# Residual written to the output early, results added by accumulating stores, and three buffer pools of the last stage laid over other places

## The chip, the cores and the metric

The kernel runs on one core of a Trainium2 chip. The time is the device time of one execution in microseconds (us). Before the change it is 1024.56 us, the median of three runs (1024.05 to 1024.94).

## The reference

Two branches are computed on the same LayerNorm of the input and added to the input itself. `x` has 2048 tokens (S) of 640 features (D); the hidden size F is 1728.

```python
xn = _layernorm(x, axis=-1)
# FNet: real part of a DFT over features and tokens
a = xn @ dft_hid_re.T ; b = xn @ dft_hid_im.T
fnet = dft_seq_re @ a - dft_seq_im @ b
# gated unit
gate = xn @ W_gate ; up = xn @ W_up
h = where(gate > 0, gate, 0) * up
return x + fnet + h @ W_down
```

All is float32.

## The kernel before

**Arithmetic.** A float32 matrix is split into a high part (rounded to the matmul's fp32r type) and a low part (the rest). `split` makes them: ScalarE (ACT) copies the high part, VectorE (DVE) subtracts it. `mm3` (lines 139 to 141) then does three matmuls of 128 x 128 by 128 x 512 for each product on TensorE (PE). The large products use a two-by-two block scheme with seven products instead of eight (names T1 to T4, S1 to S4, B11 to B22), so sums and differences of blocks are formed ahead of the matmuls, and results are added in several places afterwards.

**Stages.** Phase 1 (about 0 to 400 us) streams the sequence DFT matrices (`raw`, `tk`) over the tokens. `stream(c, name, g)` (around line 690) is one step of it: `load` issues the DMA of a 512 KB block on SyncE's queue (SP), `prepare` sums and splits, `run` multiplies. Phase 2 (about 400 to 731 us) computes `gate_up(n)` for 26 blocks n of F. A unit takes 12.2 us: it loads raw weights `z` (`Weights(n + 2)`, line 855), splits them into `gw`, runs seven block products, copies some of them from the matmul banks with ACT (`p`, `ob`, `u`: the copy must be done before PE adds the next product to the same bank), and stores the gated result `ob` to `hd` with GpSimd's queue (POOL). In the same phase, weights of the last stage are packed: loaded as `pw`, summed and stored as `wparts` (line 1060). Phase 3 (about 731 to 1019 us) multiplies the packed weights `wt` with rows `rw` and `ro` of the two branches: `project(1)`, then `project(0)`, with small further steps (`second_level`, called quads) between them.

**The last stage's steps.** `unit(name, u, first, last)` in `project` returns `load` (issue the DMA of `rw` or `ro`), `fetch` (issue the DMA of `wt`), `prepare` (differences and splits) and `run` (matmuls). `drive_last` calls `fetch`, `load`, `prepare` and `run` of successive units each some units apart (AHEAD 6, ROWS 6, READY 3). Its order is binding for SP, POOL and PE, and a scheduler places the instructions of ACT and DVE, which may land in phase 2. In phase 2 PE, DVE and ACT are bound and the scheduler places SP. Each engine works its instructions in order, and an SP or POOL instruction that waits holds back the ones behind it.

**Places.** The pools of the last stage are laid over memory of phase 2. A load into such a place waits for the last reader of what lay there before. Before the change, from the left: `low` (rows B12) over gate weights and stage, `gap`, `wts` (seven buffers for `wt`) over `r1` and part of `prep`, `lead` (six for rows B11) over the rest of `prep` and `z`, `ring2`, `raws`; from the right: `odd` (for `ro`) over gate weights, and `y`. `prep` holds the `pw` tiles until their packing stores have landed.

**Results.** The output is out = x + fnet + gated unit, transposed: 5 row blocks e of 128 features by 4 chunks of 512 tokens (q and c). `get_y` (line 1212) loads a 256 KB block of `xt`, the residual, into a place `y`. `add_y` (lines 1217 and 1219) adds one finished bank to it on DVE; when all additions to that block are done it is stored, by POOL two steps later (line 1229, `defer`) or by SP where `late` is set (line 1227). The last block is stored in two halves by ACT and SP (line 1225).

Of the kernel before, what the change touches and what calls it, by code (L numbers as in the profile page):

```python
# [10 lines left out]
OP = mybir.AluOpType  # L11
# [54 lines left out]
def fnet_reglu_kernel(  # L66
# [625 lines left out]
    def stream(c, name, g):  # L692
        t = {}
        sub = lambda o, i0, i1: nc.vector.tensor_tensor(o, i0, i1, op=OP.subtract)

        def get(m, half, o=None):
            o = raw() if o is None else o
            late["dma"] = nc.sync.dma_start(o, dft[c, m, half * NH + g]).ins
# [48 lines left out]
        todo.append((load, prepare, run, lambda: combine(c, name) if g == NH - 1 else None))  # L747
# [450 lines left out]
    y, missing, ends = {}, {}, []  # L1198

    for q in range(2):  # L1200
        for e in range(KD):
# [12 lines left out]
    def add_y(q, e, c, ps, late=False, op=OP.add, at=slice(0, CH), queue=None):  # L1214
        t = y[q, e, c][:, at]
        if op == OP.add:
            nc.vector.tensor_tensor(t, ps, t, op=OP.add)  # L1217
        else:
            nc.vector.tensor_tensor(t, t, ps, op=op)
        missing[q, e, c] -= 1  # L1220
        if missing[q, e, c] == 0 or queue is not None:
            first = (2 * q + c) * CH
            o = out[e * P : (e + 1) * P, first + at.start : first + at.stop]
            if queue is not None:
                queue.dma_start(o, t)
            elif late:
                nc.sync.dma_start(o, t)
            else:
                defer(1, lambda: nc.gpsimd.dma_start(o, t))

    def project(q):
        c0, c1 = 2 * q, 2 * q + 1
# [6 lines left out]
        def get(kind, u):  # L1239
            what, ks = UNITS[u]  # L1240
            if what == "odd":
                o = raws[kind, u] = pool("odd").tile([P, 1, CH], F32, name="ro")
            else:
                o = raws[kind, u] = pool({"B11": "lead", "B12": "low"}.get(kind, "raws")).tile([P, 2, CH], F32, name="rw")[:, : len(ks)]
# [12 lines left out]
        def unit(name, u, first, last):  # L1257
# [19 lines left out]
            def fetch():  # L1277
                if name == "B11" and (q, u) == (1, 0):
                    return
                t["w"] = w = pool("wts").tile([P, 2, 2, 3 * P], F32R, name="wt")[:, :n]  # L1280
                put = lambda o, i: nc.sync.dma_start(o.bitcast(F32), i)
                sums = wparts[:, k0 : k0 + n]
                if name in PARTS:
# [99 lines left out]
            begin = lambda: put_off.pop()()  # L1383
            return load, prepare, run, fetch

        LOADS_Y = {"B11": ((0, 0), (1, 0), (4, 1), (4, 0)) if q else ((4, 1),), "T1": ((2, 1), (3, 1)), "T2": ((0, 1), (1, 1)), "T4": ((2, 0), (3, 0))}

        def read(name):
            two = range(2)
            if name == "B11":  # L1390
# [13 lines left out]
            for e, c, key in todo:  # L1404
                if name == "T4" and q == 0 and e == 3:
                    for ps, j in ends:
                        add_y(q, e, c, ps, at=slice(j * HC, (j + 1) * HC), queue=(nc.scalar, nc.sync)[j])
                else:
                    add_y(q, e, c, B[key], late=q == 0 and name in ("T3", "T4"))

        steps = []
        for name, us in (("B11", every), ("T1", every), ("T2", every), ("B22", every[:4]), ("T3", every), ("B22", every[4:]), ("T4", every)):
            for u in us:
# [8 lines left out]
                loaded = "B11" if q and (name, u) == ("T1", 0) else name if u == 3 and (q, name) != (1, "B11") else None  # L1422
                if loaded in LOADS_Y:
                    step.append(alone((lambda which: lambda: get_y(q, *which))(LOADS_Y[loaded])))
                steps.append((step, (q, name, u)))
        return steps

    def second_level():
# [4 lines left out]
        def unit(name, g):  # L1433
# [11 lines left out]
                nc.sync.dma_start(t["r"], src)  # L1445

            def fetch():
                t["w"] = w = pool("wts").tile([P, 2, 6 * P], F32R, name="wt")[:, :n]
# [60 lines left out]

    alone = lambda f: (f, idle, idle, idle, idle)  # L1510
    quads = second_level()
    Y_AFTER = {(1, "T2", 5): ((4, 0),), (1, "T4", 5): ((0, 0), (1, 0))}
    for q in (1, 0):
        for steps, of in project(q):
            todo.extend(steps)
            if of in Y_AFTER:
                todo.append(alone((lambda which: lambda: get_y(0, *which))(Y_AFTER[of])))
# [47 lines left out]
```

## Time and profile before

One execution was profiled. All its records are of core 0.

| | us |
|---|---|
| the profiled execution's own time | 1024.17 |
| its span in the trace | 1022.4 |
| PE busy | 1016.7 |
| DVE busy | 824.4 |
| ACT busy | 455.5 |
| POOL busy | 117.3 |

The granted TensorE clock was 1.00 in all 40 slices of the span. The DMA engines were busy for 62 to 93% of the time in the windows used below. In lists of groups a row names line, engine, operation, output and input tiles and count, then the busy time and the mean of one in ns, then the idle time of the engine just before them with what ended it. In timelines the columns are start, duration, engine, line, operation, tiles, count, and in brackets the idle time before with its releaser. SPq is SyncE's sequencer issuing DMAs; a weight split stands there as `wt<-wt` on ACT, line 133, and on DVE, line 134.

### The profile page before, as it was taken

To read this page: it belongs to the slowest core of one execution; us is meant where nothing else is said; L and a number is where in the kernel's file an instruction comes from. 1 tells how busy PE (TensorE), PEld (TensorE's weight loads), DVE (VectorE), ACT (ScalarE), POOL (GpSimd) and SP (SyncE) were. 2 spreads that over 40 slices of the span, in tenths; PEclk is the share of its full clock that TensorE was granted. 3 is DMA by queue.
4 is the path that set the end of the run, shared out by engine and by line. 5 is a ranking of instruction groups with operands and counts; after the bars stand their busy time and mean duration, and the time that the engine had idled before them with its cause. 6 is when DMAs were issued, how large, how long until landed. Compare 5 with 4: busy or idle time off the path is not lost. (4 is left out here: it accounts for less than half of the span.)

```text
span 1022.4 us, 12767 instructions
## 1 busy us (share of the span) xinstructions
PE 1016.7 (99%) x4510; PEld 841.6 (82%) x4510; DVE 824.4 (81%) x1162; ACT 455.5 (45%) x588; POOL 117.3 (11%) x189
## 2 busy tenths in 40 slices
PE   9999999999999999999999999999999999999998
PEld 8888888888888888888888888888788888888887
DVE  7967976969989697788888977877487888599877
ACT  6664453333334443434445544443353454444552
POOL 2000010121110002321111111111100000000001
PEclk9999999999999999999999999999999999999999
DMA  9884744966859566764658999988698879999685
GB/s 331 320 283 157 266 147 142 332 252 205 356 200 345 218 199 217 255 231 171 234 209 282 284 311 309 308 335 266 188 399 249 257 250 328 327 314 322 216 286 167
DMA packets 113872, 267.57 MB, mean 262 GB/s; under 512 B 13104, under 2 KB 58096, under 8 KB 112176
## 3 DMA queue, kind: packets, MB, share of 16 engines
q1 hardware_dynamic: 92416, 179.03, 51.7%
q0 software_dynamic: 20960, 87.31, 24.8%
q8 instruction: 35, 0.57, 0.2%
q10 hardware_dynamic: 432, 0.43, 0.1%
q14 instruction: 29, 0.24, 0.1%
HBM read 203.26 MB, written 72.89 MB: 270 GB/s over the span
## 5 line engine op out<-in xcount | busy, mean ns | idle before, releaser
L140 PE MATMUL ps<-cb,wt 128*128 128x512 f32 (+1 forms) x407 | 158.0, 388 | 0.0
L139 PE MATMUL ps<-cb,wt 128*128 128x512 f32 (+1 forms) x407 | 157.9, 388 | 0.0
L141 PE MATMUL ps<-cb,wt 128*128 128x512 f32 (+1 forms) x407 | 157.9, 388 | 0.0
L133 ACT ACTIVATE cb<-rw 128x1024 fp32r<-128x1024 f32 (+1 forms) x94 | 89.2, 960 | 78.8 <-PE ps L141 54.7
L134 DVE TENSOR_TENSOR cb<-rw,cb 128x1024 fp32r<-128x1024 f32 (+1 forms) x94 | 102.7, 1101 | 21.6 <-ACT cb L133 20.6
L133 ACT ACTIVATE cb<-raw 128x1024 fp32r<-128x1024 f32 x64 | 67.9, 1061 | 105.1 <-PE ps L141 94.9
L134 DVE TENSOR_TENSOR cb<-raw,cb 128x1024 fp32r<-128x1024 f32 x64 | 78.1, 1221 | 31.5 <-ACT cb L133 31.1
L139 PE MATMUL ps<-xs_early,gw 128*128 128x512 f32 x260 | 101.3, 389 | 1.0 <-ACT ob L130 1.0
L140 PE MATMUL ps<-xs_early,gw 128*128 128x512 f32 x260 | 101.2, 389 | 0.0
L141 PE MATMUL ps<-xs_early,gw 128*128 128x512 f32 x260 | 101.2, 389 | 0.0
L139 PE MATMUL ps<-cb,xs_late 128*128 128x512 f32 x232 | 90.2, 389 | 0.0
L140 PE MATMUL ps<-cb,xs_late 128*128 128x512 f32 x232 | 90.2, 389 | 0.0
L141 PE MATMUL ps<-cb,xs_late 128*128 128x512 f32 x232 | 90.2, 389 | 0.0
L140 PEld LDWEIGHTS ps<-cb,wt 128*128 128x128 f32 x407 | 76.4, 188 | 15.9 <-DVE cb L134 0.3
L139 PEld LDWEIGHTS ps<-cb,wt 128*128 128x128 f32 x407 | 76.4, 188 | 15.8
L141 PEld LDWEIGHTS ps<-cb,wt 128*128 128x128 f32 x407 | 76.4, 188 | 15.8
L140 PE MATMUL ps<-cb,xs_early 128*128 128x512 f32 x226 | 87.9, 389 | 0.0
L139 PE MATMUL ps<-cb,xs_early 128*128 128x512 f32 x226 | 87.9, 389 | 0.0
L141 PE MATMUL ps<-cb,xs_early 128*128 128x512 f32 x226 | 87.9, 389 | 0.0
L130 ACT ACTIVATE gw<-z 128x1024 fp32r<-128x1024 f32 (+1 forms) x52 | 56.4, 1109 | 38.5 <-PE ps L141 22.2
L130 ACT ACTIVATE u<-ps 128x512 f32<-128x512 f32 x52 | 31.1, 597 | 88.3 <-PE ps L141 70.9
L875 DVE TENSOR_TENSOR gw<-z,gw 128x1024 fp32r<-128x1024 f32 (+1 forms) x52 | 64.8, 1284 | 1.9 <-ACT gw L130 1.8
(209 smaller groups left out, 1991.6 us busy)
## 6 DMA issues: line engine op xcount, KB each, us to landing
raw<-in_dft SPq DMA_DIRECT2D x94, 512.0 KB, 5.4
wt<-wparts SPq DMA_DIRECT2D x74, 256.0 KB, 4.4
wparts<-pw POOLq DMA_DIRECT2D x12, 1408.0 KB, 6.6
z<-in_wgu SPq DMA_DIRECT2D x26, 640.0 KB, 5.4
rw<-hd SPq DMA_DIRECT2D x27, 512.0 KB, 6.7
hd<-ob POOLq DMA_DIRECT2D x26, 512.0 KB, 4.1
wt<-wparts SPq DMA_DIRECT2D x29, 384.0 KB, 5.8
rw<-pq SPq DMA_DIRECT2D x19, 512.0 KB, 6.4
```

The costliest lines, as they stand in the source:

```text
L130: return nc.scalar.activation(o, i, AF.Copy)
L133: nc.scalar.activation(hi, src, AF.Copy)
L134: return nc.vector.tensor_tensor(lo, src, hi.bitcast(F32), op=OP.subtract)
L139: nc.tensor.matmul(ps, wh, mh, start=first, stop=False, skip_group_check=more)
L140: nc.tensor.matmul(ps, wh, ml, start=False, stop=False, skip_group_check=more)
L141: nc.tensor.matmul(ps, wl, mh, start=False, stop=last, skip_group_check=more)
L875: tt(self.w[:, 1, cs], self.z[:, cs], self.w[:, 0, cs].bitcast(F32), op=OP.subtract)
```

## The change

Three things are edited.

1. The residual goes to the output in phase 1: five copies of 1 MB from `xt` to `out`, on SP's queue, in the load step of five units of the first chunk (`XT_AT`). 18 of the 20 loads of `y` are dropped. The first result for a block is now copied from its bank by ACT (with factor −1 where it is subtracted), later ones are added by DVE as before, and the finished block is stored by POOL with an adding DMA. Two blocks, (q 0, e 2, c 0) and (q 0, e 3, c 0), are still loaded (`load_plain`) and stored plainly, the last of them in two halves.
2. Two stores of q = 0, which SP issued, are issued by POOL.
3. The pools of the last stage get other places. From the left now: `odd`, `y0`, `gap`, `wts0` (five buffers), `wts1` (two), `y1`, `lead0` (five), `ring2`, `lead1` (one), `low`, `raws` (16 instead of 15); from the right `y2`. `in_two` hands out the buffers of `wts` and `lead` in turn over their two pools.

```diff
+XT_AT = (("T3", 1), ("T3", 3), ("T4", 0), ("T4", 1), ("T4", 2))
...
         def load():
+            if c == 0 and (name, g) in XT_AT:
+                e = XT_AT.index((name, g))
+                nc.sync.dma_start(out[e * P : (e + 1) * P], xt[e * P : (e + 1) * P])
...
-    for n, b, side in (("low", 6, "left"), ("gap", 1, "left"), ("wts", AHEAD + 1, "left"), ("lead", 6, "left"), ("ring2", 4, "left"), ("raws", 15, "left"),
-                       ("odd", 4, "right"), ("y", 1, "right")):
+    for n, b, side in (("odd", 4, "left"), ("y0", 1, "left"), ("gap", 1, "left"), ("wts0", 5, "left"), ("wts1", AHEAD - 4, "left"),
+                       ("y1", 1, "left"), ("lead0", 5, "left"), ("ring2", 4, "left"), ("lead1", 1, "left"), ("low", 6, "left"),
+                       ("raws", 16, "left"), ("y2", 1, "right")):
...
+    Y_AT = {n: "y0" if i < 8 else "y1" if i < 9 else "y2" for i, n in enumerate("001 101 401 41 01 11 21 31 20 30 000 100 400".split())}
+    turns = {"wts": [0, AHEAD + 1], "lead": [0, 6]}
+
+    def in_two(name):
+        turns[name][0] += 1
+        return pool(name + str(int((turns[name][0] - 1) % turns[name][1] >= 5)))
...
-    def get_y(q, *which):
-        for e, c in which:
-            own = f"{q}" if e in (0, 1, 4) and c == 0 else ""
-            y[q, e, c] = t = pool("y").tile([P, CH], F32, name=f"y{e}{c}{own}")
-            nc.sync.dma_start(t, xt[e * P : (e + 1) * P, (2 * q + c) * CH : (2 * q + c + 1) * CH])
...
+    def add_y(q, e, c, ps, op=OP.add, at=slice(0, CH), queue=None):
+        o = out[e * P : (e + 1) * P, (2 * q + c) * CH + at.start : (2 * q + c) * CH + at.stop]
+        missing[q, e, c] -= 1
+        if (q, e, c) not in y:
+            t = place_y(q, e, c)
+            nc.scalar.activation(t, ps, AF.Copy, scale=1.0 if op == OP.add else -1.0)
         else:
-            nc.vector.tensor_tensor(t, t, ps, op=op)
...
+            t = y[q, e, c][:, at]
+            if op == OP.add:
+                nc.vector.tensor_tensor(t, ps, t, op=OP.add)
+            else:
+                nc.vector.tensor_tensor(t, t, ps, op=op)
+        if queue is not None:
+            queue.dma_start(o, t)
+        elif missing[q, e, c] == 0:
+            if (q, e, c) in PLAIN:
                 nc.sync.dma_start(o, t)
             else:
-                defer(1, lambda: nc.gpsimd.dma_start(o, t))
+                defer(1, lambda: nc.gpsimd.dma_start(o, t, accum_op=OP.add))
...
-                t["w"] = w = pool("wts").tile([P, 2, 2, 3 * P], F32R, name="wt")[:, :n]
+                t["w"] = w = in_two("wts").tile([P, 2, 2, 3 * P], F32R, name="wt")[:, :n]
```

The change moves instructions at three places that the prediction speaks of. The lists show an engine's instructions in program order; a number at the end of a tile's name only tells tiles apart.

At the end of phase 2, SP's queue before the change: the first weights, then rows and weights of the next units, and the first `ro`.

```order
L1281 DMA wt_5793<-wparts_94 128x2x384
L1253 DMA rw_5795<-pq2_88 128x1024
L1253 DMA rw_5797<-pq2_88 128x1024
L1281 DMA wt_5799<-wparts_94 128x384
L1253 DMA rw_5801<-pq2_88 128x512
L1281 DMA wt_5803<-wparts_94 128x2x384
L1255 DMA rw_5805<-hd1_91 128x2x512
L1281 DMA wt_5812<-wparts_94 128x384
L1251 DMA ro_5814<-hd1_91 128x512
L1281 DMA wt_5821<-wparts_94 128x2x384
```

And after it, the same queue at this place. `rw_5812` waits for the packing store of the second to last `pw` tile instead of the last one, `ro_5831` for the last product of unit 24 instead of the products of unit 25.

```order
L859 DMA z_5482<-in_wgu 128x1280
L1271 DMA rw_5812<-pq2_88 128x1024
L1271 DMA rw_5814<-pq2_88 128x1024
L1299 DMA wt_5816<-wparts_94 128x384
L1271 DMA rw_5818<-pq2_88 128x512
L1299 DMA wt_5820<-wparts_94 128x2x384
L1273 DMA rw_5822<-hd1_91 128x2x512
L1299 DMA wt_5829<-wparts_94 128x384
L1269 DMA ro_5831<-hd1_91 128x512
L1299 DMA wt_5838<-wparts_94 128x2x384
L1273 DMA rw_5840<-hd1_91 128x2x512
L1299 DMA wt_5847<-wparts_94 128x2x384
```

The rows and weights between the last `z` and `ro` keep their order. The first weights (`wt_5793` before) have left this place. They stand in unit 18 now, on SP behind its `z` load:

```order
L1045 DMA pw_4890<-in_wd 128x128
L1046 DMA pw_4890<-in_wd 128x256
L859 DMA z_4987<-in_wgu 128x1280
L1299 DMA wt_5810<-wparts_94 128x2x384
L1044 DMA pw_4989<-in_wd 128x256
```

ACT in that unit, first before and then after the change: the split of these weights now stands between the weights of the next unit and the copy `ob`.

```order
L130 ACTIVATE gw_4967<-z_4883 128x1024
L130 ACTIVATE gw_4967<-z_4883 128x1152
L130 ACTIVATE ob_4965<-ps_4935 128x512
L130 ACTIVATE u2_4962<-ps_4933 128x512
L130 ACTIVATE u3_4963<-ps_4933 128x512
```
```order
L131 ACTIVATE gw_4972<-z_4888 128x1024
L131 ACTIVATE gw_4972<-z_4888 128x1152
L134 ACTIVATE wt_5810<-wt_5810 128x2x384
L131 ACTIVATE ob_4970<-ps_4940 128x512
L131 ACTIVATE u2_4967<-ps_4938 128x512
```

Nothing else in that unit's order on ACT is changed.

ACT at the end of phase 2, first before, then after: three splits stand ahead of unit 25's `ob` in both, and two more now stand behind it, ahead of the copies `u2` and `u3`. Line numbers after the change are higher by 1 to 18.

```order
L130 ACTIVATE p1_5635<-ps_5611 128x512
L133 ACTIVATE wt_5799<-wt_5799 128x384
L133 ACTIVATE wt_5803<-wt_5803 128x2x384
L133 ACTIVATE wt_5812<-wt_5812 128x384
L130 ACTIVATE ob_5639<-ps_5613 128x512
L130 ACTIVATE u2_5636<-ps_5611 128x512
L130 ACTIVATE u3_5637<-ps_5611 128x512
```
```order
L131 ACTIVATE p1_5640<-ps_5616 128x512
L134 ACTIVATE wt_5816<-wt_5816 128x384
L134 ACTIVATE wt_5820<-wt_5820 128x2x384
L134 ACTIVATE wt_5829<-wt_5829 128x384
L131 ACTIVATE ob_5644<-ps_5618 128x512
L134 ACTIVATE wt_5838<-wt_5838 128x2x384
L131 ACTIVATE u2_5641<-ps_5616 128x512
L134 ACTIVATE wt_5847<-wt_5847 128x2x384
L131 ACTIVATE u3_5642<-ps_5616 128x512
```

The splits of `wt_5838` and `wt_5847` answer to those of `wt_5821` and `wt_5830`, which stood behind all of unit 25's copies.

More of the change, by code (lines that the diff above doesn't have):

```diff
@@ L1197, in fnet_reglu_kernel @@
     fixed = [bank() for _ in range(8)]
-    y, missing, ends = {}, {}, []
+    Y_AT = {n: "y0" if i < 8 else "y1" if i < 9 else "y2" for i, n in enumerate("001 101 401 41 01 11 21 31 20 30 000 100 400".split())}
[3 more added lines that the diff above has]
+        return pool(name + str(int((turns[name][0] - 1) % turns[name][1] >= 5)))
+    y, missing, ends, PLAIN = {}, {}, [], ((0, 2, 0), (0, 3, 0))
     for q in range(2):
@@ L1206, in fnet_reglu_kernel, with place_y, load_plain @@
     missing[0, 3, 0] += 2
-    def get_y(q, *which):
-        for e, c in which:
-            own = f"{q}" if e in (0, 1, 4) and c == 0 else ""
-            y[q, e, c] = t = pool("y").tile([P, CH], F32, name=f"y{e}{c}{own}")
-            nc.sync.dma_start(t, xt[e * P : (e + 1) * P, (2 * q + c) * CH : (2 * q + c + 1) * CH])
[L1214 to L1217, printed above, removed]
-        else:
-            nc.vector.tensor_tensor(t, t, ps, op=op)
[L1220 to L1226, printed above, removed]
+    def place_y(q, e, c):
+        own = f"{q}" if e in (0, 1, 4) and c == 0 else ""
+        y[q, e, c] = t = pool(Y_AT[f"{e}{c}{own}"]).tile([P, CH], F32, name=f"y{e}{c}{own}")
+        return t
+    def add_y(q, e, c, ps, op=OP.add, at=slice(0, CH), queue=None):
[4 more added lines that the diff above has]
+            nc.scalar.activation(t, ps, AF.Copy, scale=1.0 if op == OP.add else -1.0)
+        else:
+            t = y[q, e, c][:, at]
[7 more added lines that the diff above has]
+            if (q, e, c) in PLAIN:
                 nc.sync.dma_start(o, t)
             else:
-                defer(1, lambda: nc.gpsimd.dma_start(o, t))
+                defer(1, lambda: nc.gpsimd.dma_start(o, t, accum_op=OP.add))
+    def load_plain():
+        for q, e, c in PLAIN:
+            nc.sync.dma_start(place_y(q, e, c), xt[e * P : (e + 1) * P, (2 * q + c) * CH : (2 * q + c + 1) * CH])
     def project(q):
@@ L1243, in get @@
             else:
-                o = raws[kind, u] = pool({"B11": "lead", "B12": "low"}.get(kind, "raws")).tile([P, 2, CH], F32, name="rw")[:, : len(ks)]
+                o = raws[kind, u] = (in_two("lead") if kind == "B11" else pool("low" if kind == "B12" else "raws")).tile([P, 2, CH], F32, name="rw")[:, : len(ks)]
             col, row = int(kind in ("B12", "B22")), int(kind in ("B21", "B22"))
@@ L1384, in unit @@
             return load, prepare, run, fetch
-        LOADS_Y = {"B11": ((0, 0), (1, 0), (4, 1), (4, 0)) if q else ((4, 1),), "T1": ((2, 1), (3, 1)), "T2": ((0, 1), (1, 1)), "T4": ((2, 0), (3, 0))}
         def read(name):
@@ L1408, in read @@
                 else:
-                    add_y(q, e, c, B[key], late=q == 0 and name in ("T3", "T4"))
+                    add_y(q, e, c, B[key])
         steps = []
@@ L1421, in project @@
                     step.append((l, p, r, (lambda name: lambda: read(name))(kind) if last else idle, f))
-                loaded = "B11" if q and (name, u) == ("T1", 0) else name if u == 3 and (q, name) != (1, "B11") else None
-                if loaded in LOADS_Y:
-                    step.append(alone((lambda which: lambda: get_y(q, *which))(LOADS_Y[loaded])))
+                if (q, name, u) == (0, "T4", 3):
+                    step.append(alone(load_plain))
                 steps.append((step, (q, name, u)))
@@ L1447, in fetch @@
             def fetch():
-                t["w"] = w = pool("wts").tile([P, 2, 6 * P], F32R, name="wt")[:, :n]
+                t["w"] = w = in_two("wts").tile([P, 2, 6 * P], F32R, name="wt")[:, :n]
                 put = lambda o, i: nc.sync.dma_start(o.bitcast(F32), i)
@@ L1515, in fnet_reglu_kernel @@
             todo.extend(steps)
-            if of in Y_AFTER:
-                todo.append(alone((lambda which: lambda: get_y(0, *which))(Y_AFTER[of])))
             if of == (1, "T2", 6):
```

1 line of the change is left out of this document (removed).

## The prediction

> **What bounds the kernel now.** I read the page first: the busy list, then its costliest groups with the idle time before each.
>
> ```profile
> span 1022.4 us, 12767 instructions
> PE 1016.7 (99%) x4510; PEld 841.6 (82%) x4510; DVE 824.4 (81%) x1162; ACT 455.5 (45%) x588; POOL 117.3 (11%) x189
> L139 PE MATMUL ps<-xs_early,gw 128*128 128x512 f32 x260 | 101.3, 389 | 1.0 <-ACT ob L130 1.0
> ```
>
> TensorE (PE) is busy for 1016.7 of 1022.4 us. The change keeps all matmuls, so it can win only what PE does not fill: the start, a tail, and one hole, which the third row names: 1.0 us, behind ScalarE's (ACT's) copy `ob`. Next I read PE's timeline around the hole.
>
> ```profile
> 717.87 0.39 PE L141 MATMUL ps<-sets_b,gw 128*128 128x512 f32 x1
> 719.23 0.50 PE L139 MATMUL ps<-xs_early,gw 128*128 128x512 f32 x1 [0.97 <-ACT ob L130]
> 721.41 0.39 PE L139 MATMUL ps<-sets_b,gw 128*128 128x512 f32 x1
> ```
>
> It is one wait, at the end of phase 2 (the second row names it with 0.97 of the 1.0 us). A matmul starts every 1016.7 / 4510 = 0.23 us, so 719.23 − 717.87 − 0.23 = 1.13 us are lost. ACT's timeline says why, and SP's, whose queue issues the loads, says what was late before that:
>
> ```profile
> 714.68 0.53 ACT L133 ACTIVATE wt<-wt 128x384 fp32r<-128x384 f32 x1 [3.14 <-DMA wt<-wparts]
> 716.33 0.85 ACT L133 ACTIVATE wt<-wt 128x768 fp32r<-128x768 f32 x1 [1.12 <-DMA wt<-wparts]
> 718.17 0.52 ACT L133 ACTIVATE wt<-wt 128x384 fp32r<-128x384 f32 x1 [0.99 <-DMA wt<-wparts]
> 718.60 0.58 ACT L130 ACTIVATE ob<-ps 128x512 f32<-128x512 f32 x1
> ```
> ```profile
> 683.87 1.94 SPq L1281 DMA_DIRECT2D wt<-wparts  x1
> 705.09 1.69 SPq L1253 DMA_DIRECT2D rw<-pq  x2
> 709.11 0.47 SPq L1281 DMA_DIRECT2D wt<-wparts  x1
> 731.80 0.33 SPq L1251 DMA_DIRECT2D ro<-hd  x1
> ```
> ```profile
> 687.78 0.54 POOL L1060 DMA_DIRECT2D wparts<-pw  x1 [7.27 <-DMA z<-in_wgu]
> 699.98 0.56 POOL L1060 DMA_DIRECT2D wparts<-pw  x1 [6.86 <-DVE z L861]
> ```
> ```profile
> SPq L1253 <- DMA wparts<-pw: 17.8, 1, 17.8
> ```
>
> ACT works in order: three weight splits stand ahead of the `ob` copy and wait for their loads until 718.17. Without them the copy would start when its product ends: 1.16 us before PE wants it, as in unit 18 below, or 716.9. Those loads stand on SP between 705.09 and 709.11, because the row load ahead of them waited 17.8 us for the last packing store, issued at 699.98, to leave the place (`prep`) that the row overlays.
>
> **The change, part by part.**
>
> *1. Places at the boundary: removes the hole.* In the new order the first two `rw`, the three weight loads and their rows are issued behind the last `z` of phase 2 and wait for the store of 687.78, one unit sooner, and for a DVE instruction of that unit. One unit is 699.98 − 687.78 = 12.2 us, so they go out that much earlier, by 697, and even the slow loads of this place:
>
> ```profile
> wt<-wparts SPq DMA_DIRECT2D x1, 384.0 KB, 8.4
> ```
>
> (the one 384 KB weight load issued in 705 to 710, issue to landing) have landed by 706, ten before `ob` is due. Value −1.13; bounds 0 (another wait takes over) and −1.36 (the whole step from one start to the next). That is term one.
>
> *2. A new wait and a moved split at the same boundary.* `ro` now lies over gate weights and waits for the last product that reads them:
>
> ```profile
> 712.43 0.39 PE L141 MATMUL ps<-xs_early,gw 128*128 128x512 f32 x1
> ```
>
> It ends at 712.82. Queued behind `ro` on SP are a 384 KB `wt`, `rw`, `wt`, `rw`. Before they went out only after 732, so no product of phase 2 could wait for them; now the split of that first `wt` stands on ACT between `ob` and the next copy `u`, which PE needs for its matmul at 721.41, hole taken off 720.28. The copy takes 0.60 and the split 0.85 less an overlap of 0.05 to 0.1, so the load must land by 718.85. It is issued near 713.25: 5.6 us are allowed. Its rows:
>
> ```profile
> wt<-wparts SPq DMA_DIRECT2D x29, 384.0 KB, 5.8
> wt<-wparts SPq DMA_DIRECT2D x3, 384.0 KB, 8.7
> ```
>
> (the page's median, and three in 731 to 735). 5.8 costs 0.2 us of PE, 8.7 costs 3.1, and a load under 5.6 costs nothing. Fewer loads are in flight with it than at 705 or 731 (four against seven), so I take +0.4, near the median row. The second `wt` stands behind one more copy and is taken at nothing.
>
> *3. The first `wt` fetched five units earlier.* It stood at 683.87, and its split ran after `ob` and a `u` of unit 24, with nothing due behind it. Its new place is free early, so SP issues it right behind the `z` load of unit 18, and its split stands ahead of that unit's `ob`:
>
> ```profile
> 624.51 0.42 SPq L855 DMA_DIRECT2D z<-in_wgu  x1
> ```
> ```profile
> 631.26 0.60 ACT L130 ACTIVATE ob<-ps 128x512 f32<-128x512 f32 x1 [1.97 <-PE ps L141]
> ```
> ```profile
> 632.42 0.39 PE L139 MATMUL ps<-xs_early,gw 128*128 128x512 f32 x1
> ```
> ```profile
> z<-in_wgu SPq DMA_DIRECT2D x1, 640.0 KB, 5.8
> wt<-wparts SPq DMA_DIRECT2D x1, 384.0 KB, 6.2
> ```
>
> The last fence is such a pair, a `z` and the `wt` right behind it, issued in 683.3 to 684. With 6.2 us from an issue near 625.0 the weights land at 631.2, in the very moment when `ob` could start (631.26); split to 632.05, copy to 632.6, against PE's 632.42. Free if it lands by 631.0; +0.2 at 6.2; +2.7 at 8.7. I take +0.3.
>
> [...]
>
> *4. Five 1 MB copies of the residual into the output, on SP in phase 1.* The trace has no such copy. SP's longest wait, in that phase, and three windows:
>
> ```profile
> SPq L698 <- DVE cb L134: 177.4, 46, 24.1
> ```
> ```profile
> 50.00:100.00 50.00, 50.00 (x223) 41.39 (x222) 34.99 (x55) 26.86 (x39) 1.06 (x2) 1.00 0.65 224
> 100.00:200.00 100.00, 100.00 (x443) 82.81 (x442) 82.67 (x94) 42.01 (x51) 11.54 (x20) 1.00 0.62 214
> 850.00:950.00 100.00, 100.00 (x442) 82.62 (x441) 78.88 (x93) 49.79 (x64) 2.16 (x4) 1.00 0.93 322
> ```
>
> The last columns are DMA share and GB/s. 224 GB/s at a share of 0.65 is 345 at full share: an estimate of 3.0 us for 1.05 MB, 6.1 if reading and writing count apart, 15 to 30 us for five. Free in the first two windows are 17.5 + 38 = 55 us. The loads of that phase wait for places (177.4 us of SP for this line alone), not for bytes, and PE is full in both windows. Value 0; without that cover a copy delays the load behind it by up to 6 us.
>
> *5. Phase 3: 18 residual loads go, 18 adds become copies, stores accumulate.*
>
> ```profile
> y<-in_xt SPq DMA_DIRECT2D x20, 256.0 KB, 6.8
> L1217 DVE TENSOR_TENSOR y<-ps,y 128x512 f32<-128x512 f32 (+1 forms) x43 | 27.4, 670 | 4.6 <-PE ps L141 3.5 <-PE ps L1360 1.1
> L130 ACT ACTIVATE u<-ps 128x512 f32<-128x512 f32 x52 | 31.1, 597 | 88.3 <-PE ps L141 70.9
> ```
>
> VectorE (DVE) loses 18 × 0.67 = 12.1 us, ACT gains 18 × 0.60 = 10.7; both beside a full PE, worth nothing unless a bank is released late. 18 loads leave the DMA engines, five of them in the window with a share of 0.93. The 18 stores turn into accumulating ones on POOL. Landing times of its lines, minimum, median, maximum, first the plain 256 KB stores, then the accumulating 512 KB stores of phases 2 and 3:
>
> ```profile
> DMA to landing us min/median/max: 3.8/4.8/7.5
> ```
> ```profile
> DMA to landing us min/median/max: 5.1/6.9/9.2
> ```
>
> So at most 2.1 us later in the median and 1.7 in the maximum, with half the bytes. Who waits for a store? In the new order only ACT's copies of q = 0 into places that q = 1 used, and their stores are a stream of units older. Even the saturated window should see no more traffic: a load and a store become one store that reads and writes. Value 0, bounds −0.3 and +3; the gain is this one, the only other place in phase 3 where PE's weight loads wait:
>
> ```profile
> PEld ps L140 <- DVE cb L134: 0.3, 1, 0.3
> ```
>
> *6. Tail.*
>
> ```profile
> 1003.54 3.63 POOL L1229 DMA_DIRECT2D out<-y  x6 [27.69 <-DVE y L1217]
> 1018.45 0.28 PE L141 MATMUL ps<-cb,wt 128*128 128x256 f32 x1
> 1019.21 0.35 SPq L1225 DMA_DIRECT2D out<-y  x1
> ```
> ```profile
> out<-y SPq DMA_DIRECT2D x1, 128.0 KB, 2.2
> ```
>
> The last stores stay plain: 1019.21 + 2.2 = 1021.4 ends the work. Six accumulating stores from 1003.5, issued by 1009.5 at most, land by 1018.7 even at 9.2. Value 0.
>
> **Sum** against the profiled execution's own 1024.17 us (1.8 outside its span): −1.13 + 0.4 + 0.3 = −0.43, 1023.74. That execution lies 0.39 under the median of the runs, 1024.56, so for the median I add it: **1024.1**, rounded to 1024.0.
>
> **The rivals.**
> - *Loads late at the new places (slower).* Both moved splits stand ahead of copies that PE needs, with 5.6 and 6.05 us allowed. One us over costs PE one us at each. At 8.4 us (705 to 710): +2.8 and +2.4, less 1.13, is +4.1: 1028.6. Slower than the bound once both take over 7.2 us. For: 8.4 and 8.7 at this boundary. Against: those landed in a crowd of seven or more loads, which part 1 dissolves.
> - *The hole closes and nothing opens.* Loads of 5.5 us or less: −1.13, with the 0.3 of phase 3 −1.4: 1023.1. For: 5.8 is a median, half land sooner.
> - *Accumulating stores disturb the saturated window (slower).* From 835 to 881 eight of them; if each holds up the loads behind it by the 2.1 us between the medians, one or two of the places near 880 and 893 let PE wait 2 us each: +3, 1027. For: share 0.93. Against: five loads leave there.
> - *A 1 MB copy delays phase 1's loads (slower).* 6 us once, less 2 or more of lead: +4, 1028. Against: PE has no wait there.
> - *The change doesn't move the boundary.* The place of the first `rw` stays bound to the last packing store: 1024.6.
>
> **How the numbers follow.** Forecast (1023.5 to 1025.0) 0.53, hole closed only 0.19, nothing moved 0.05, loads late 0.13, stores 0.06, copies 0.04. 0.2%, about what a measurement of this kernel can tell from no change, is 2.05 us: faster than 1022.5 lies beyond the whole hole and the 0.3, hence 0.05 for a surprise, taken from the second case. Slower than 1026.6: most of the last three, 0.20. Within: 0.75. The range runs from 1022.7 (hole, 0.3 and spread of the runs) to 1026.8, where the late cases begin to count; the forecast's own is 1023.5 to 1025.0.
>
> **What would show it.** Part 1: no wait of PE for `ob` near 718, `rw` and `wt` issued by 700. Part 2: SP waiting for PE until about 713, the `wt` behind it landing between 718 and 720; if later, a wait of PE for `u` near 720. Part 3: a weight split of ACT near 631 and a wait of PE for `ob` near 632 of a few tenths. Part 4: no wait of PE from 50 to 200. Part 5: PE busy as before from 731 to 1003, landing of accumulating stores 5 to 7 us. Part 6: the last store landing 3 us after the last matmul. A PE wait of over 1 us anywhere else would make the prediction wrong.

## The result, and the profile after

The changed kernel takes 1037.82 us (median of four runs, 1035.35 to 1039.35) against 1024.75 for the kernel before: 1.0125 times as long, with a 95% interval of 1.0102 to 1.0147. The prediction was 1024.0, with a range to 1026.8. It was slower, and by more than any rival had been priced.

The profiled execution took 1035.35 us. The page's busy lines and the group that had the hole before:

```profile
span 1033.6 us, 12749 instructions
PE 1020.1 (99%) x4510; PEld 841.5 (81%) x4510; DVE 813.4 (79%) x1144; ACT 463.4 (45%) x606; POOL 124.2 (12%) x191
L140 PE MATMUL ps<-xs_early,gw 128*128 128x512 f32 x260 | 101.5, 390 | 2.9 <-ACT ob L131 2.9
```

The span grew by 11.2 us, PE's busy time by only 3.4: the matmuls are the same 4510, so PE waits 7.8 us more, and some of its matmuls are slower. Its waits (line, releaser, sum, count and longest):

```profile
PE ps L140 <- ACT ob L131: 2.9, 1, 2.9
PE ps L140 <- ACT cb L134: 2.2, 2, 1.1
PE ps L141 <- DVE cb L135: 2.0, 4, 0.5
PE ps L140 <- DVE y L1234: 1.2, 1, 1.2
```

Because both kernels run the same matmuls in nearly the same order, the start of the k-th matmul can be compared between the two traces. The difference grows in few places only. This table is worked out from the two traces: a step is the time from one matmul's start to the next after the change, less the same time before it. Places are given at the time in the kernel before.

| where | step, us | what PE waited for |
|---|---|---|
| 194.5 to 197.7 | 1.26 + 0.69 + 0.70 = 2.65 | `cb` of phase 1 |
| 632.4 | 3.04 | ACT's `ob` in unit 18 |
| just behind it | 1.71 | nothing: matmuls at a granted clock of 0.50 |
| 719.2 | −1.13 | the old hole is gone |
| 880.1 and 881.4 | 1.25 + 1.36 = 2.61 | `cb`, and the bank that `y` reads |
| 893.2 | 0.54 | `cb` |
| 929 to 935 | 0.88 | `cb` |
| the rest, small | 0.83 | |
| last matmul, 1018.45 to 1029.58 | 11.13 | |

Three separate losses, then: phase 1, unit 18, and phase 3 around 880 to 935. The profiled execution is the shortest of the four; what the other three lost beyond it, 1.7 to 4.0 us, is in no trace. I show the lines for each loss.

**Unit 18.** ACT, SP and the landings there, in the changed kernel:

```profile
628.13 0.38 SPq L1299 DMA_DIRECT2D wt<-wparts  x1
```
```profile
z<-in_wgu SPq DMA_DIRECT2D x1, 640.0 KB, 6.8
wt<-wparts SPq DMA_DIRECT2D x1, 384.0 KB, 9.0
```
```profile
637.14 0.84 ACT L134 ACTIVATE wt<-wt 128x768 fp32r<-128x768 f32 x1 [4.78 <-DMA wt<-wparts]
637.89 0.58 ACT L131 ACTIVATE ob<-ps 128x512 f32<-128x512 f32 x1
```

The split stands ahead of `ob` as foreseen, but its load needs 9.0 us instead of 6.2. Then PE's windows (busy and count of PE, PEld, DVE, ACT, POOL, then the granted clock, DMA share and GB/s):

```profile
638.50:640.00 1.50, 1.47 (x6) 1.25 (x7) 0.48 (x1) 0.46 (x1) 0.00 (x0) 0.97 0.24 81
640.00:643.40 3.40, 3.40 (x9) 2.62 (x9) 1.68 (x4) 0.00 (x0) 0.00 (x0) 0.51 0.85 226
643.40:650.00 6.60, 6.60 (x30) 5.45 (x29) 4.97 (x12) 4.05 (x5) 0.54 (x1) 1.00 0.62 249
```

After the wait PE runs at full speed for 1.4 of the 1.5 us of the first row, then 3.4 us at a granted clock of 0.51, then at 1.00 again. The nine matmuls of the second row take the time of some fifteen.

**Phase 1.** DVE in the changed kernel (first fence), and before (second):

```profile
190.58 0.69 DVE L567 TENSOR_TENSOR sa<-ps,sa 128x512 f32<-128x512 f32 x1 [1.71 <-PE ps L142]
191.30 0.69 DVE L570 SCALAR_TENSOR_TENSOR sb<-sb,sa 128x512 f32<-128x512 f32 x1
191.94 0.69 DVE L567 TENSOR_TENSOR sa<-ps,sa 128x512 f32<-128x512 f32 x1
192.66 0.69 DVE L570 SCALAR_TENSOR_TENSOR sb<-sb,sa 128x512 f32<-128x512 f32 x1
193.27 1.22 DVE L695 TENSOR_TENSOR raw<-raw,tk 128x1024 f32<-128x1024 f32 x1
```
```profile
189.56 1.22 DVE L694 TENSOR_TENSOR raw<-raw,tk 128x1024 f32<-128x1024 f32 x1
190.70 1.22 DVE L134 TENSOR_TENSOR cb<-raw,cb 128x1024 fp32r<-128x1024 f32 x1
191.83 1.28 DVE L566 TENSOR_TENSOR sa<-ps,sa 128x512 f32<-128x512 f32 x2
```
```profile
194.61 1.06 ACT L134 ACTIVATE cb<-raw 128x1024 fp32r<-128x1024 f32 x1 [7.00 <-DVE raw L695]
```

DVE now does the four `sa` and `sb` additions ahead of the difference `raw - tk`. They wait 1.71 us for a product of PE, and the difference that PE's next weights come from stands in line behind them. ACT (third fence, changed kernel) stands idle for 7.0 us until it is there. Before, the difference of 189.56 was made ahead of the additions. The difference of 193.27 has no wait of its own, so no load that it needs was late, and the last of the five copies had landed by 181.4: the order of DVE's work makes PE wait here, not the copies' traffic.

**Phase 3.** The DMA queues in equal stretches of 70 us, 828 to 898 before and 835 to 905 after (queue, packets, MB, share of 16 engines). Before:

```profile
q1 hardware_dynamic: 12610, 18.76, 79.6%
q0 software_dynamic: 720, 2.36, 9.0%
...
wt<-wparts SPq DMA_DIRECT2D x13, 256.0 KB, 4.4
```

After:

```profile
q1 hardware_dynamic: 11347, 16.41, 69.0%
q0 software_dynamic: 1296, 2.36, 26.9%
...
wt<-wparts SPq DMA_DIRECT2D x13, 256.0 KB, 6.4
```

POOL's queue (q0) carries nothing but the nine result stores. Nine plain ones take 9.0% of 70 us, 0.70 us of all 16 engines each; nine adding ones take 26.9%, 2.1 us each, with 64 packets more each. The two queues' share together rises from 88.6 to 95.9% though fewer bytes are loaded, and the 256 KB weights land 2 us later. PE's two largest waits there, and the work of ACT and DVE that they go back to:

```profile
887.92 0.47 PE L140 MATMUL ps<-cb,wt 128*128 128x512 f32 x1 [1.09 <-ACT cb L134]
890.74 0.50 PE L140 MATMUL ps<-cb,wt 128*128 128x512 f32 x1 [1.19 <-DVE y L1234]
```
```profile
886.10 0.53 ACT L134 ACTIVATE wt<-wt 128x384 fp32r<-128x384 f32 x1 [1.30 <-DMA wt<-wparts]
886.53 1.99 ACT L134 ACTIVATE cb<-rw 128x1024 fp32r<-128x1024 f32 x2
887.74 2.35 DVE L135 TENSOR_TENSOR cb<-rw,cb 128x1024 fp32r<-128x1024 f32 x2
890.01 0.68 DVE L1234 TENSOR_TENSOR y<-ps,y 128x512 f32<-128x512 f32 x1
```

The first wait goes back to a late load: a weight split that waited for its DMA stands on ACT ahead of the `cb` that PE needs. Before, that split stood at 877.14, which is 883.7 with the 6.6 us added by which the changed kernel is behind there: 2.4 us sooner. The second wait has a further cause, the order on DVE. Before:

```profile
878.78 1.22 DVE L134 TENSOR_TENSOR cb<-rw,cb 128x1024 fp32r<-128x1024 f32 x1
879.91 0.68 DVE L1217 TENSOR_TENSOR y<-ps,y 128x512 f32<-128x512 f32 x1
880.51 1.22 DVE L134 TENSOR_TENSOR cb<-rw,cb 128x1024 fp32r<-128x1024 f32 x1
```

One `cb` stood ahead of the addition to `y` and one behind it. Now both stand ahead, and the addition, which frees the bank that PE wants, comes 1.14 us later.

### The profile page after: what moved, and what is told of

It reads as the page before. It is cut to its first block, busy times and chain, and to the rows that moved or that the text cites. A ratio compares the mean times of both kernels' runs of the same rounds, so it can differ in the third digit from the quotient of the medians.

```text
span 1033.6 us, 12749 instructions
## 1 busy us (share of the span) xinstructions
PE 1020.1 (99%) x4510; PEld 841.5 (81%) x4510; DVE 813.4 (79%) x1144; ACT 463.4 (45%) x606; POOL 124.2 (12%) x191
## 5 line engine op out<-in xcount | busy, mean ns | idle before, releaser
L135 DVE TENSOR_TENSOR cb<-rw,cb 128x1024 fp32r<-128x1024 f32 (+1 forms) x94 | 102.4, 1100 | 27.4 <-ACT cb L134 26.9
L135 DVE TENSOR_TENSOR wt<-wt 128x768 fp32r<-128x768 f32 (+5 forms) x64 | 45.1, 713 | 38.5 <-ACT wt L134 38.2
```

Of the source, the lines that this page charges most:

```text
L135: return nc.vector.tensor_tensor(lo, src, hi.bitcast(F32), op=OP.subtract)
```

## The experiments

All times are medians of the runs of that kernel, with the ratio to the kernel before, which took 1024.2 to 1024.3 us beside them, and its 95% interval. What is called a step or wait at a place is from the matmul starts of that kernel's one trace, given at the place's time in the kernel before.

**1. The first weight load of phase 3 tied to a later place.**

```diff
-                nc.sync.dma_start(self.z2[:, :NRAW], wgu[n % NF])
+                late["z"] = nc.sync.dma_start(self.z2[:, :NRAW], wgu[n % NF]).ins
...
+                if (q, name, u) == (1, "B11", 1):
+                    with tc.issue_after(late["z"]):
+                        put(w[:, :, 1], wparts[:, k0 : k0 + n, O1 : O1 + 3 * P])
+                    return
```

> The changed kernel, but the first weight load of phase 3 is tied behind the last z load of phase 2, so that its split no longer stands ahead of unit 18's ob. Theory (the changed kernel's loss has three separate places: 2.7 us at 194 to 198, 4.9 at 632 to 643, 4.4 at 880 to 935, less 1.1 for the closed hole): the wait for ob near 638 and the slow matmuls behind it go, 1037.8 - 4.9 = 1032.9, and 719 stays closed. Rival (the load only meets another crowd and makes another ob wait): no gain, 1037.

1031.27 us, 1.0068 (1.0053 to 1.0083). The wait at 632 and the slow matmuls are gone, 6.5 us less in the median (3.8 between the two profiled executions; that of the changed kernel is the shortest of its four). But both sides had a part of the truth: the split now stands ahead of unit 23's `ob`, and a wait of 1.22 us appears there (693.6). A split ahead of a copy that PE needs is free only if its load lands in time.

**2. The copies of the residual in units 3 to 7 of phase 2.**

```diff
-            if c == 0 and (name, g) in XT_AT:
-                e = XT_AT.index((name, g))
-                nc.sync.dma_start(out[e * P : (e + 1) * P], xt[e * P : (e + 1) * P])
...
+    def copy_xt(e):
+        with tc.issue_after(late["z"]):
+            nc.sync.dma_start(out[e * P : (e + 1) * P], xt[e * P : (e + 1) * P])
+
+    for e in range(KD):
+        loads[3 + e].append((lambda e: lambda: copy_xt(e))(e))
```

> The changed kernel, but the five 1 MB copies of the residual are issued in units 3 to 7 of phase 2 behind the z loads; the order of PE and DVE in phase 1 is then the order before the change. Theory: the three waits at 194 to 198 come from the order of DVE there and go: 1037.8 - 2.7 = 1035.1, and no wait in phase 2 from the copies, whose DMA share is 0.55 to 0.66 there. Rival (the copies' traffic made the waits): a PE wait of 1 us or more appears in units 3 to 8 instead.

1034.49 us, 1.0074 (1.0044 to 1.0104). No wait at 194 to 198 and none in units 3 to 8: the five megabytes cost nothing there. The median falls by 3.3, as far as it can be told: the single times lie between 1027.0 and 1034.8. The likely reason is the wait at 632: it is 2.46 to 6.50 us in the traces that have it, and the times of runs 2, 3 and 6, which keep it, spread over 7.6 to 9.1 us (run 4: 1.5), those of the kernels without it over 2.8 at most.

**3. Plain instead of adding stores.** The residual is left out of the 18 blocks.

```diff
-                defer(1, lambda: nc.gpsimd.dma_start(o, t, accum_op=OP.add))
+                defer(1, lambda: nc.gpsimd.dma_start(o, t))
```

> The changed kernel with the 18 adding stores made plain ones; this leaves the residual out of those 18 blocks. Order and places stay. Theory (an adding store takes 2.1 us of all 16 DMA engines against 0.7, and in the full window around 880 it makes weight loads late): the waits at 880 to 935 go, 1037.8 - 4.4 = 1033.4. Rival (ACT's copies of first results, or the new places, make the weights late): the waits stay, 1037.

1034.8 us, 1.0087 (1.006 to 1.0115), 1029.1 to 1036.7. The median does not settle it, since in the profiled execution the wait at 632 grew to 6.50 us (its load took 12.9 us). The trace does: after 719 a step of 0.38 is the largest that is left, against 4.0 us in all in the changed kernel. Its queue in 840 to 910:

```profile
q0 software_dynamic: 720, 2.36, 8.8%
```

The nine stores are back to 0.7 us of the engines each. So the waits of phase 3 need the adding; ACT's copies and the places do not make them by themselves.

**4. The 18 first copies on DVE instead of ACT.**

```diff
-            nc.scalar.activation(t, ps, AF.Copy, scale=1.0 if op == OP.add else -1.0)
+            if op == OP.add:
+                nc.vector.tensor_copy(t, ps)
+            else:
+                nc.vector.tensor_scalar(t, ps, -1.0, None, op0=OP.mult)
```

> The changed kernel with the 18 first copies on DVE instead of ACT. Theory (adding stores): the waits at 880 to 935 stay, 1037.8 within 1.5. Rival (ACT's copies stand in front of splits): they go, 1033.4.

1038.78 us, 1.0143 (1.0126 to 1.016). The waits at 880 to 893 stay (0.92, 1.37, 1.03): the rival is out.

**5. The five copies alone, added to the kernel before.**

```diff
         def load():
+            if c == 0 and (name, g) in XT_AT:
+                e = XT_AT.index((name, g))
+                nc.sync.dma_start(out[e * P : (e + 1) * P], xt[e * P : (e + 1) * P])
```

> The kernel before, with nothing added but the five 1 MB copies of the residual in phase 1 (the output is written over later as before). The scheduler then orders DVE and PE near 190 as in the changed kernel. Theory: waits of PE at 194.5, 194.9 and 197.7, 2.7 us in all, 1024.3 + 2.7 = 1027.0; nothing else moves. Rival (the waits need the rest of the change): 1024.3.

1027.62 us, 1.0034 (1.0022 to 1.0046). Steps of 1.26 and 0.69 at 194.5 and 194.9 are there, and behind them eight slow matmuls (1.5 us), which also stand in the profiled execution of some other kernels with the copies, but not in that of the changed kernel. The step at 197.7 is not there. DVE's order is that of the changed kernel; with the copies in phase 2 (run 2) or without them it is that of the kernel before. Five DMAs on SP changed what DVE does first.

**6. The new places alone.** The residual is loaded, added and stored as before; the pools are those of the change, and `y` uses the places of `Y_AT`.

```diff
-                o = raws[kind, u] = pool({"B11": "lead", "B12": "low"}.get(kind, "raws")).tile([P, 2, CH], F32, name="rw")[:, : len(ks)]
+                o = raws[kind, u] = (in_two("lead") if kind == "B11" else pool("low" if kind == "B12" else "raws")).tile([P, 2, CH], F32, name="rw")[:, : len(ks)]
...
-                t["w"] = w = pool("wts").tile([P, 2, 2, 3 * P], F32R, name="wt")[:, :n]
+                t["w"] = w = in_two("wts").tile([P, 2, 2, 3 * P], F32R, name="wt")[:, :n]
```

> The kernel before with the places of the changed kernel for wts, lead, low, odd and raws, but with the residual loaded and added on DVE and stored plainly as before. Theory: the hole at 718 is closed (-1.1) and the split in front of unit 18's ob costs 4 to 8.5 us with the slow matmuls behind it: 1027.2 to 1031.7; no wait of PE over 0.5 us after 731. Rival (the new places make phase 3's loads late): waits of PE at 880 to 893 of 2 us or more, 1030 to 1035.

1030.89 us, 1.0061 (1.0037 to 1.0084), 1025.2 to 1034.3. A wait of 5.87 us at 632 with slow matmuls behind it (its load took 12.2 us), the hole at 719 closed (−1.13), a wait of 0.66 at 726 that was not expected, nothing behind it. The places by themselves bring both the gain foreseen and the loss in unit 18, and no loss in phase 3.

**7. The copies and adding stores alone, with the places of the kernel before.** The edit is to the changed kernel:

```diff
-    for n, b, side in (("odd", 4, "left"), ("y0", 1, "left"), ("gap", 1, "left"), ("wts0", 5, "left"), ("wts1", AHEAD - 4, "left"),
...
+    for n, b, side in (("low", 6, "left"), ("gap", 1, "left"), ("wts", AHEAD + 1, "left"), ("lead", 6, "left"), ("ring2", 4, "left"), ("raws", 15, "left"),
+                       ("odd", 4, "right"), ("y", 1, "right")):
...
-                t["w"] = w = in_two("wts").tile([P, 2, 2, 3 * P], F32R, name="wt")[:, :n]
+                t["w"] = w = pool("wts").tile([P, 2, 2, 3 * P], F32R, name="wt")[:, :n]
```

> The changed kernel with the places of the kernel before: early copies, first copies on ACT and adding stores alone. Theory: 1024.3 + 2.7 (phase 1) + 4.4 (adding stores at 880 to 935) = 1031.4, the hole at 718 stays, and there is no wait near 632. Rival (places and adding stores only do harm together): 1027.

1030.83 us, 1.0064 (1.005 to 1.0077). Waits at 194 and 195 with slow matmuls behind them, the hole at 719 (0.39 larger), waits of 0.35, 1.36 and 0.66 at 880, 881 and 893, none at 632. Phase 3 lost 2.4 us by these waits where 4.4 were expected. The two halves of the change add up, as far as the spread of run 6 lets one tell: 6.7 + 6.7 = 13.4 in the medians against 13.1.

**8. The new places, and the first weights' split behind unit 25's last copy.** The edit on top of run 6:

```diff
-        copy(u3, b1)
+        late["u3"] = copy(u3, b1).ins
...
-                        split(w[:, :, 0], w[:, :, 1], w[:, :, 1].bitcast(F32))
+                        with tc.issue_after(late["u3"]) if (q, name, u) == (1, "B11", 1) else ExitStack():
+                            split(w[:, :, 0], w[:, :, 1], w[:, :, 1].bitcast(F32))
```

> As pools_only, and the split of the first weights of phase 3 is ordered behind unit 25's last copy u3, where the weights have long landed. Theory: only the closed hole is left: 1024.3 - 1.1 = 1023.2, or 1022.9 with the 0.3 at 893. Rival (the weight load that now goes out near 713 makes the u copy at 720 late): 1023.5 to 1026, with a PE wait near 720.

1024.15 us, 0.9998 (0.9988 to 1.0007): the rival, at another load than it named. The wait at 632 is gone, the hole at 719 closed, and 1.28 us are lost at 726. PE's waits, ACT there, and the load:

```profile
PE ps L139 <- ACT u L130: 1.1, 1, 1.1
```
```profile
725.08 0.84 ACT L133 ACTIVATE wt<-wt 128x768 fp32r<-128x768 f32 x1 [5.29 <-issue]
725.83 0.58 ACT L130 ACTIVATE u<-ps 128x512 f32<-128x512 f32 x1
```
```profile
wt<-wparts SPq DMA_DIRECT2D x1, 384.0 KB, 9.1
```

It is the second of the weight loads issued behind `ro`. It took 9.1 us, from 715.8 to 724.9, and its split held the copy `u3` back. The first, issued at 713.5, took 4.9 and cost nothing.

**9. The same with all three splits behind `u3`.**

```diff
-                        with tc.issue_after(late["u3"]) if (q, name, u) == (1, "B11", 1) else ExitStack():
+                        with tc.issue_after(late["u3"]) if (q, name) == (1, "B11") and u in (1, 5, 6) else ExitStack():
```

> As pools_split_placed, with the splits of the two weight loads issued near 713 also ordered behind unit 25's u3, so that no copy of phase 2 stands behind a load that is still on its way. Theory (places are worth the closed hole alone, and the wait at 726 came from the second of these splits): 1024.2 - 1.1 = 1023.1, no PE wait of over 0.3 us between 700 and 1018. Rival (the splits, now in a row behind u3, make phase 3's first products late): a wait near 735, 1024 or more.

1023.06 us, 0.9989 (0.9979 to 0.9998) over eleven runs. The rival's wait at 735 did not come: from 700 to 1018 PE's waits have no entry. In the list of the whole span one is left, the start:

```profile
PE ps L121 <- DVE warm L117: 1.1, 1, 1.1
```

This kernel is faster than the changed kernel and, by 1.1 us, than the kernel before: the closed hole and no more.

**10 and 11. The changed kernel with the copies in phase 2 and the three splits behind `u3`; and the same with plain stores.** To the changed kernel the edits of runs 2 and 9 are made, and in the second run also that of run 3:

```diff
+        with tc.issue_after(late["z"]):
+            nc.sync.dma_start(out[e * P : (e + 1) * P], xt[e * P : (e + 1) * P])
...
+                        with tc.issue_after(late["u3"]) if (q, name) == (1, "B11") and u in (1, 5, 6) else ExitStack():
...
-                defer(1, lambda: nc.gpsimd.dma_start(o, t, accum_op=OP.add))
+                defer(1, lambda: nc.gpsimd.dma_start(o, t))
```

> The changed kernel with the copies of the residual in phase 2 and the three splits behind u3: what is left of the change are the places and the adding stores. Theory: 1024.2 - 1.1 + 2.5 to 4.5 (adding stores, waits at 880 to 935) = 1025.6 to 1027.6. Rival (the waits at 880 depended on what ran late before): 1023.1.

> As all_but_order with plain stores (the residual is left out of 18 blocks): the lighter traffic of phase 3 without the adding. Theory: no wait at 880 to 935 over 0.4 us, 1024.2 - 1.1 = 1023.1, no faster than pools_three_splits, since 18 loads less are worth nothing beside a full PE.

1026.75 us, 1.0022 (1.0012 to 1.0033), and 1023.63, 0.9992 (0.9983 to 1.0001). The first has waits of 1.49, 1.38, 0.49 and 0.32 at 880 to 935, 3.7 in all, though nothing ran late before: the waits of phase 3 don't need the other two losses. Between the two kernels only the adding differs, and it costs 3.1 us in the medians. The second fell short of its expectation in one point: a wait of 0.99 at 881 is left, for a bank that DVE's `y` had not read yet, so the lighter traffic did not give a clean phase 3, and the kernel is not faster than run 9. Its DVE has the order of the changed kernel there, both `cb` ahead of the addition, where run 9 has the order of the kernel before. In run 3, with the same order, 0.38 of it is left. No run puts the old order back under adding stores, so what the order is worth in the changed kernel stays open.

**12. PE idle on purpose, in the kernel before.** In eleven units of phase 2 ACT makes useless copies ahead of `ob`; the results are the same.

```diff
+        for _ in range(DELAY.get(n, 0)):
+            copy(u2, p1)
         copy(ob[:, c1], b4)
```

> The kernel before with useless ACT copies ahead of ob in eleven units of phase 2 (7, 8, 9, 10, 8, 9, 10, 8, 9, 12 and 7 of 0.5 to 0.6 us in units 2 to 22), which make PE wait there. Theory (a wait of PE over about 2 us is followed by some ten matmuls at half speed, a short one is not): steps of 1 to 5 us, and behind those over 2 us eight to twelve matmuls of 0.43 us instead of 0.23. Rival (the slow matmuls at 640 belong to the load, not to the wait): all at 0.23.

1084.15 us in one run. Two waits of 1.92 us were followed by matmuls at full speed. So was one of two waits of 2.58 us, and the other was not. All seven of 3.2 to 6.0 us were followed by slow ones. In all eight cases these were 6 to 14 matmuls, which cost 1.4 to 2.9 us. A longer wait did not make more of them: 6.02 us cost 1.4 behind it, 3.24 us cost 2.7. The two waits of 2.58, ending at 466.2 and 652.2:

```profile
466.20:471.00 4.80, 4.80 (x14) 3.84 (x15) 1.46 (x3) 0.42 (x1) 0.00 (x0) 0.64 0.03 12
652.20:657.00 4.80, 4.76 (x21) 3.95 (x22) 2.12 (x5) 1.50 (x3) 0.00 (x0) 1.00 0.68 181
```

The clock of the first stretch is 0.64, with 14 matmuls where the second has 21 at a clock of 1.00. Matmuls at the lower clock start 0.43 us apart (468.33 to 468.76), the others 0.23.

## Why the prediction was wrong, step by step

**Part 1 was right in its value.** The hole at 719 closed, and gave −1.13 in the trace of every kernel with the new places. Its landing times were wrong: the weights that were to be there by 706 landed up to 11 us after their issue in the changed kernel, and up to 18 us in run 10. It held because the loads had some 19 us, from 698 to 717 in the times of run 10, and there with only 0.18 us to spare between the last split and `ob`. That part of it is luck.

**Part 2 cost nothing in the changed kernel, where +0.4 was taken, but it watched the wrong load.** SP waited for PE until 720.7 and issued as foreseen; the first `wt` landed 3.5 us after its issue, not 5.8, and the second 6.5 us after. Neither cost anything:

```profile
725.30 0.84 ACT L134 ACTIVATE wt<-wt 128x768 fp32r<-128x768 f32 x1
726.16 0.60 ACT L131 ACTIVATE u<-ps 128x512 f32<-128x512 f32 x1
728.74 0.85 ACT L134 ACTIVATE wt<-wt 128x768 fp32r<-128x768 f32 x1 [1.98 <-DMA wt<-wparts]
729.61 0.60 ACT L131 ACTIVATE u<-ps 128x512 f32<-128x512 f32 x1
```

But the second split, "taken at nothing", is the one that costs when its load is slow (9.1 us and 1.28 lost in run 8, 9.2 us and 0.66 in run 6). The step looked at the first of two loads in a queue, and the second took longer in all three traces.

**Part 3 is the term that was mis-sized: +0.3 taken, 4.75 measured in the profiled execution.** The mechanism was described rightly: split ahead of `ob`, late load, PE waits. Two figures failed. The load was priced at 6.2 us by such a pair at 683, though unit 18 is another crowd: there a packing store of 1.4 MB follows the load of 628.13 by 1.5 us, at 683 by 3.9 (683.87 and 687.78). POOL's queue moved 1.84 MB between 628.1 and 637.1, while this load was on its way, and 0.59 MB between 683.9 and 690.1. The DMA share was 1.03 and 0.96 in these two stretches (packets counted where they start). That this is why the load was late is an inference; no run moves the store alone.

```profile
629.65 0.55 POOL L1064 DMA_DIRECT2D wparts<-pw  x1 [7.18 <-DMA pw<-in_wd]
```

In the kernels with this place it took 9.0 (changed kernel), 8.5 (run 2), 12.9 (run 3), 10.9 (run 4) and 12.2 us (run 6). The upper end of part 3, +2.7 at 8.7 us, was no end. And "One us over costs PE one us" held for the wait itself: the load landed 3.05 us after the last free moment (631.0, or 634.07 in the changed kernel, which is 3.07 behind there), and the wait cost 3.04. But it left out what followed this wait: 1.7 us lost at a granted clock of 0.50.

**Part 4 failed in its reasoning.** Value 0 was taken because the loads had room, and they had: no load is late at 194 in the changed kernel, and run 2 moves the same five megabytes in phase 2 with no wait. What the part left out is that new instructions change the order in which the scheduler places work that they have nothing to do with. Four additions moved ahead of a difference that PE's next weights need, and the part speaks of the copies as transfers only, not of DVE's order or of what the moved instructions wait for. It cost 2.65 us in the changed kernel; in run 5, where slow matmuls follow, 3.4 in the median. The order of DVE at 881 in phase 3 changed in the same way.

**Part 5 failed in "the saturated window should see no more traffic".** A plain load and a plain store were counted as equal to one adding store. Queue shares say 0.70 us of the engines for a plain store and 2.1 for an adding one. For a plain load of 256 KB an estimate is 0.78 us, from SP's 18.76 MB in 79.6% of 70 us: the adding store alone (2.1) is dearer than load and store together (0.78 + 0.70). Landing times were the wrong view for this price. They were taken from transfers that add from DRAM to DRAM (`grown<-hd` and `grown<-pq`, L1145), not from SBUF, and came out nearly as foreseen even so:

```profile
DMA to landing us min/median/max: 5.5/7.1/9.9
```

The price stands in what the other transfers lose. This was the third rival, at 0.06. Its mechanism was right, loads behind the stores landing some 2 us later, and so was its price of 3: 3.1 us between runs 10 and 11 (the waits themselves add up to 3.7 in run 10 and to 4.0 in the changed kernel, with the order on DVE in them).

**Part 6 was right.** The last matmul and the last store's issue, with a tail as long as before:

```profile
1029.58 0.28 PE L142 MATMUL ps<-cb,wt 128*128 128x256 f32 x1
1030.35 0.35 SPq L1238 DMA_DIRECT2D out<-y  x1
```

The main fault stands behind the single ones: three places were each valued at 0 or nearly 0, each with a rival of small chance, and the rivals were treated as excluding one another. All three came at once: loads late, stores dear, and the copies (by another way than the one named). The sum of their prices would have been +11. That this is near the 13.1 measured is in part luck: the price of the late loads was meant for two splits, of which one cost nothing and the other 4.75, and that of the copies for late loads, which did not come.

Two slips in the sums changed nothing: they give 1024.1, not 1024.0, and the late loads pass 1026.6 when both take 7.4 us, not 7.2.

## What to carry to other kernels

Where one engine is full, a change can only win the holes in it, but each edit may open a new one: ask of every instruction that is moved what it waits for, not how long it takes, and read the new order on every engine, also in places that the edit doesn't touch. Price a load by the crowd that it will be in, its last member first, and what a DMA costs the others by the share of the engines that it takes, not by its landing time. Put work that depends on a fresh load behind the copies that the full engine needs (run 9), and add the prices of independent rivals instead of choosing among them.

## What the runs showed of the hardware

Some waits of PE were followed by slow matmuls. In the changed kernel, after the wait of 3.04 us, PE went on at full speed for 1.4 us and then ran for 3.41 us (639.91 to 643.32) at a granted clock of 0.50; in run 12 the slow stretches held 6 to 14 matmuls. In the traces of these runs all waits of 3 us and more (3.04 to 6.50) showed it, of three near 2.5 us (2.46 and twice 2.58) two, and single ones of 1.92 us and less none; the pair of 1.26 and 0.69 us at 195, 1.3 us apart, showed it in the traces of runs 3, 5 and 7 and not in those of the changed kernel and of runs 1 and 4.

So the length of a wait alone does not tell: of the two waits of 2.58 us in run 12 one was followed by a granted clock of 0.64 in 466.2 to 471.0, the other by 1.00 in 652.2 to 657.0. Nor did a longer wait cost more behind it: 6.02 us cost 1.4, 3.24 us cost 2.7. What makes the difference was not shown.

In the full window nine adding stores of 256 KB from SBUF to DRAM took 26.9% of 70 us of all 16 DMA engines, 2.1 us each (changed kernel), and nine plain ones 9.0%, 0.70 us each (kernel before).
